# An MM-DiT block on one core: the first stage rebuilt (scale columns and V weights loaded in interleaved row pieces, V accumulated in six open banks, layernorm on two engines), and the text branch's modulation moved from the Q stage to the K stage

## Chip, cores, metric

One core of a Trainium2 chip. The metric is the time of one execution in microseconds (us), as the device reports it; lower is better. Times are medians over all runs of a job; ratios use its fast-state runs alone. The span of a profile is about 2 us shorter than the reported time.

## The reference, cut to what matters

```python
B, Ni, Nt, D = 2, 256, 32, 1152            # bf16
mod_i = silu(c) @ wmod_img                 # shift, scale, gate columns of the image branch
mod_t = silu(c) @ wmod_txt                 # the same for the text branch
hi = layernorm(x_img) * (1 + sci) + shi
ht = layernorm(x_txt) * (1 + sct) + sht
qkvi, qkvt = hi @ wqkv_img, ht @ wqkv_txt
p = softmax(concat(qt, qi) @ concat(kt, ki).T * D ** -0.5)
a = p @ concat(vt, vi)
out_i = x_img + gai * (ai @ wo_img)
out_t = x_txt + gat * (at @ wo_txt)
```

All 14 weight blocks of 1152 x 1152 (2.65 MB each, 37.2 MB) are read once; with the activations and the scratch rows the profile counts 39.5 MB read from HBM.

## The kernel before: what the change and the argument touch

There are three things to know. First, the image branch: layernorm, transposes on TensorE, a pass that multiplies by the scale (three engines), then V, then shift, then Q, then K.

```python
w_sc_i = load_w(wmod_img, D)                              # one DMA of 2.65 MB each
w_v_i = load_w(wqkv_img, 2 * D, splits=(CH, 2 * CH))      # by columns
w_sh_i = load_w(wmod_img, 0)
w_q_i = load_w(wqkv_img, 0)
w_sh_t = load_w(wmod_txt, 0)                              # text shift, text scale ...
w_sc_t = load_w(wmod_txt, D)
w_k_i = load_w(wqkv_img, D)                               # ... ahead of the image K weights
# [cut]
for i in range(NIT):
    layernorm(x_i[:, i, :], P, xn_i[:, i, :])             # VectorE statistics, ScalarE sqrt
    ... transposes, ScalarE copies the result to hT_i
for b in range(B):
    h_pass(b, shift=False)                                # hT_i *= 1 + scale, three engines
```

Second, the text branch's shift and scale are computed as rows (`mod_rows`). A row has to reach 64 partitions. The kernel stores it to a scratch tensor in DRAM and reads it back broadcast. Both DMAs are issued by GpSimd:

```python
def mod_rows(w_blk, si, add_one=False, lhs=None):
    ...                                                   # 36 matmuls, PSUM copied to g_sb
    for b in range(B):
        nc.gpsimd.dma_start(gsc[si, b, :]..., g_sb[b:P:32, :])          # store
def txt_rows_scale():
    mod_rows(w_sc_t, 1, add_one=True)
    for k in range(2):                                    # k = 0 shift, k = 1 scale
        for b in range(B):
            nc.gpsimd.dma_start(mb_t[b * NT:(b + 1) * NT, k, :], gsc[k, b, :].partition_broadcast(NT))
def txt_modulate():                                       # VectorE
    mul(xn_t, xn_t, mb_t[:, 1, :]); add(xn_t, xn_t, mb_t[:, 0, :])
def txt_transposes(): ...                                 # TensorE, 9 transposes, then hT_t
```

Third, where these pieces stand among the nine groups of nine matmuls that make up Q and K:

```python
qk_img(w_q_i, 0, hooks={0: txt_ln, 3: txt_rows_shift, 6: txt_rows_scale})
qk_img(w_k_i, 1, hooks={5: txt_modulate, 7: txt_transposes})
```

## Time and profile before

| | before |
|---|---|
| time, median of 3 | 130.49 us |
| span of the profile | 128.9 us |
| TensorE (PE) busy | 110.3 us, 86% |
| Q's first matmul | 40.4 us |
| K's last group ends | 78.6 us |

The second part of the page shows the span in 40 equal slices: TensorE's busy share in tenths, the granted TensorE clock in tenths, and the DMA traffic in GB/s.

```profile
PE   0005799999999999999999999799989999999960
PEclk9999999999999999999999999999999999999999
GB/s 59 409 415 357 381 401 406 409 411 412 357 405 411 406 409 410 408 413 379 412 371 372 372 374 374 388 412 405 409 405 411 335 14 90 6 92 0 92 97 46
```

TensorE has nothing to do for 11 us and then is busy to the end. The loads run near 400 GB/s to about 100 us. So the kernel is bound by TensorE, after a start that waits for x, layernorm and the first scale columns.

The chain of waits (start, length, what), from Q to the end of the text branch, shows a TensorE that never waits for the text branch:

```profile
40.46 2.05 PE ps L218 x9
...
74.29 0.36 PE tpt L293 x9
...
75.25 3.40 PE ps L218 x15
78.65 4.32 PE ps L305 x148
82.96 0.93 issue
```

L218 is the Q and K matmuls, L293 the text transposes, L305 the text Q and K. The timeline of GpSimd shows the trips through DRAM; L259 is a store to scratch and L279 a read-back:

```profile
48.41 1.15 POOL L259 DMA_DIRECT2D mod_scratch<-g_sb  x2 [0.50 <-DVE g_sb L129]
53.44 1.09 POOL L279 DMA_DIRECT2D mb_t<-mod_scratch  x2 [3.88 <-DMA mod_scratch<-g_sb]
55.56 1.17 POOL L259 DMA_DIRECT2D mod_scratch<-g_sb  x2 [1.03 <-DVE g_sb L253]
61.27 1.15 POOL L279 DMA_DIRECT2D mb_t<-mod_scratch  x2 [4.54 <-DMA mod_scratch<-g_sb]
```

The scale rows' matmuls end at 54.8 us. The store is issued at 55.6, the read-back at 61.3, and its data are in at 66.9 (the later of the two copies). The text transposes stand at 74.2 in TensorE's order, so some 6 us of slack are left after 1.5 us of VectorE work.

### The profile page before, as it was taken

The numbers are of one execution on the slowest core, as the hardware profiler recorded it, in microseconds if no ns is written. First come the engines' busy times: TensorE is split into PE (matmuls) and PEld (weight loads), VectorE is DVE, ScalarE is ACT, GpSimd is POOL, SyncE is SP. The second block draws the span as 40 slices with busy tenths as digits, with TensorE's granted clock in tenths as the row PEclk, the third lists the DMA queues.
The fourth block names the chain that finished last, engine by engine and source line by source line (L and its number), as shares of the span: only waits on it lengthen the run. The fifth ranks groups of instructions, "written<-read, shape, count | busy, mean of one in ns | idle before, by whom it ended". The sixth has DMA issues, their size and how long they took to land.

```text
span 128.9 us, 2643 instructions
## 1 busy us (share of the span) xinstructions
PE 110.3 (86%) x1123; PEld 69.3 (54%) x1128; DVE 56.7 (44%) x147; ACT 33.4 (26%) x71; POOL 19.8 (15%) x48
## 2 busy tenths in 40 slices
PE   0005799999999999999999999799989999999960
PEld 0004685665865454544444447778767755555550
DVE  0099965111357610231026211225987656545670
ACT  3054584221133211101111031143675400010000
POOL 8910132000034133330300000011200000000000
PEclk9999999999999999999999999999999999999999
DMA  3999999999999999999999999999999802020221
GB/s 59 409 415 357 381 401 406 409 411 412 357 405 411 406 409 410 408 413 379 412 371 372 372 374 374 388 412 405 409 405 411 335 14 90 6 92 0 92 97 46
DMA packets 19703, 41.05 MB, mean 318 GB/s; under 512 B 811, under 2 KB 3403, under 8 KB 19691
## 3 DMA queue, kind: packets, MB, share of 16 engines
q1 hardware_dynamic: 18875, 39.75, 81.7%
q0 software_dynamic: 672, 1.06, 2.2%
q8 instruction: 9, 0.15, 0.5%
q10 hardware_dynamic: 144, 0.07, 0.2%
q14 instruction: 3, 0.02, 0.0%
HBM read 39.53 MB, written 1.35 MB: 317 GB/s over the span
## 4 chain that ended last, share of the span: by engine, by line
PE 79%; DVE 8%; DMA 4%; ACT 3%; issue 2%; DVEq 0%
PE ps L218 27%; PE ps L227 14%; PE ps L426 14%; PE aps L377 5%; PE gps L249 5%; DMA x_i<-in_x_img_dram 4%; PE ps L305 4%; PE tp L158 3%; PE mps L164 2%; DVE stats L142 2%; PE ps L446 2%; PE sps L336 2%; ACT hT_i L159 1%; DVE pb L328 1%; DVE pb L326 1%
## 5 line engine op out<-in xcount | busy, mean ns | idle before, releaser
L218 PE MATMUL ps<-hT_i,t 128*128 128x512 bf16 x157 | 35.4, 379 | 0.3
L218 PEld LDWEIGHTS <-t 128*128 128x128 bf16 x162 | 15.5, 98 | 18.9 <-issue 0.7
L227 PE MATMUL ps<-t,hT_i 128*128 128x384 bf16 x108 | 18.9, 338 | 0.0
L426 PE MATMUL ps<-t,aT 128*128 128x384 bf16 x108 | 17.9, 326 | 0.0
L227 PEld LDWEIGHTS <-hT_i 128*128 128x128 bf16 x108 | 10.9, 102 | 7.4 <-issue 0.3
L426 PEld LDWEIGHTS <-aT 128*128 128x128 bf16 x108 | 10.6, 98 | 6.8
L429 DVE TENSOR_TENSOR tmp<-ps,gb 128x384 bf16<-128x384 f32 x12 | 6.7, 558 | 7.3 <-PE ps L426 7.3
L129 DVE CAST qkT<-ps 128x512 bf16<-128x512 f32 (+1 forms) x5 | 3.3, 665 | 13.6 <-PE ps L218 11.8
L118 PE MATMUL sT_ps<-ident,s_140 18*128 18x18 bf16 x1 | 0.2, 192 | 10.5 <-DVE s_140 L116 10.5
L259 POOL DMA_DIRECT2D mod_scratch<-g_sb x8 | 4.7, 591 | 27.4 <-DVE g_sb L129 26.4
L129 DVE CAST v_i<-ps 128x384 bf16<-128x384 f32 x6 | 3.3, 557 | 11.5 <-PE ps L227 11.5
L205 DVE TENSOR_SCALAR qkT<-ps 128x512 bf16<-128x512 f32 (+1 forms) x5 | 3.3, 665 | 11.5 <-PE ps L218 8.7
L131 ACT CAST qkT<-ps 128x512 bf16<-128x512 f32 (+1 forms) x6 | 3.3, 542 | 19.5 <-PE ps L218 16.4
L142 DVE BATCH_NORM_STATS2 stats<-x_i 128x6 f32<-128x384 bf16 x12 | 5.9, 531 | 5.3 <-DMA x_i<-in_x_img_dram 5.3
L207 ACT ACTIVATE qkT<-ps 128x512 bf16<-128x512 f32 (+1 forms) x6 | 3.3, 553 | 17.9 <-PE ps L218 16.2
L377 PE MATMUL aps<-pT,v_i 128*128 128x288 bf16 x36 | 6.6, 286 | 0.7 <-ACT pT L131 0.6
L182 DVE TENSOR_SCALAR hT_i<-hT_i,mod_img 128x256 bf16<-128x256 bf16 x20 | 5.8, 346 | 0.7 <-ACT hT_i L159 0.6
L305 PE MATMUL ps<-hT_t,t 128*128 128x64 bf16 x162 | 5.0, 193 | 0.9 <-issue 0.9
L118 PEld LDWEIGHTS <-s_140 18*128 18x128 bf16 x1 | 0.1, 100 | 10.5 <-DVE s_140 L116 10.5
L158 PE MATMUL tp<-ident,xn_i 128*128 128x128 bf16 x36 | 4.5, 310 | 1.3 <-DVE xn_i L148 0.9
L305 PEld LDWEIGHTS <-t 128*128 128x128 bf16 x162 | 4.9, 98 | 1.3 <-issue 1.0
L159 ACT COPY hT_i<-tp 128x640 bf16<-128x640 bf16 (+1 forms) x8 | 4.7, 642 | 2.8 <-PE tp L158 2.8
(88 smaller groups left out, 127.0 us busy)
## 6 DMA issues: line engine op xcount, KB each, us to landing
t<-in_wmod_img_dram SPq DMA_DIRECT2D x3, 2592.0 KB, 17.8
t<-in_wmod_txt_dram SPq DMA_DIRECT2D x3, 2592.0 KB, 16.9
t<-in_wqkv_txt_dram SPq DMA_DIRECT2D x3, 2592.0 KB, 24.1
t<-in_wqkv_img_dram SPq DMA_DIRECT2D x2, 2592.0 KB, 22.1
t<-in_wo_img_dram SPq DMA_DIRECT2D x1, 2592.0 KB, 23.5
t<-in_wo_txt_dram SPq DMA_DIRECT2D x1, 2592.0 KB
t<-in_wqkv_img_dram SPq DMA_DIRECT2D x1, 1728.0 KB, 16.5
x_i<-in_x_img_dram SPq DMA_DIRECT2D x1, 1152.0 KB, 5.5
```

The source lines that it names most:

```text
L129: last_dve[0] = nc.vector.tensor_copy(out_ap, in_ap)
L142: nc.vector.bn_stats(stats[0:np_, k, :], x_ap[:, k * CH:(k + 1) * CH])
L158: nc.tensor.transpose(tp[:, kt - k0, :], xn_i[:, i, kt * P:(kt + 1) * P], ident[:])
L159: nc.scalar.copy(hT_i[:, k0:k1, i * P:(i + 1) * P], tp[:, 0:k1 - k0, :])
L182: nc.vector.tensor_scalar(sl, sl, ap, None, op0=op)
L218: nc.tensor.matmul(ps[:], lhsT=wq[:, kt, j * P:(j + 1) * P], rhs=hT_i[:, kt, :], start=(kt == 0), stop=(kt == KT - 1))
L227: nc.tensor.matmul(ps[:], lhsT=hT_i[:, kt, i * P:(i + 1) * P], rhs=w_v_i[:, kt, cch * CH:(cch + 1) * CH], start=(kt == 0), stop=(kt == KT ...
L249: nc.tensor.matmul(gps[32 * g:32 * g + 32, :], lhsT=lhs[:, kt, :], rhs=w_blk[:, kt, g * VC:(g + 1) * VC], start=(kt == 0), stop=(kt == KT ...
L305: nc.tensor.matmul(ps[:, j - j0, :], lhsT=wq[:, kt, j * P:(j + 1) * P], rhs=hT_t[:, kt, :], start=(kt == 0), stop=(kt == KT - 1))
L377: nc.tensor.matmul(aps[:], lhsT=lhsT, rhs=pT[:, kj, :], start=(kj == 0), stop=(kj == 2))
L426: nc.tensor.matmul(ps[0:np_, :], lhsT=lhsT_of(dt), rhs=w_o[:, dt, cs], start=(dt == 0), stop=(dt == KT - 1))
L429: nc.vector.tensor_mul(tmp[0:np_, :], ps[0:np_, :], gate_ap[:, cs])
```

## The change

The intent is to start V earlier. Scale columns and V rows arrive in alternating pieces. As soon as a piece of scale columns is known, the transposed tokens are scaled while they leave PSUM. V accumulates piece by piece in six PSUM banks that stay open. Layernorm is shared between ScalarE and VectorE, dummy matmuls should raise TensorE's clock beforehand, and the order of TensorE is fixed ("pinned"). The new scaled copy takes room, so weight buffers go from six to five. K's weights now come ahead of the text weights, and with them the text rows move into K. The diff, cut to its core:

```diff
-    wpool = ctx.enter_context(tc.tile_pool(name="w", bufs=6))
+    wpool = ctx.enter_context(tc.tile_pool(name="w", bufs=5))
-    ps_mm = ... bufs=4 ; ps_tr bufs=2 ; ps_sm bufs=2
+    ps_mm = ... bufs=6 ; ps_tr bufs=2
+    pin = tc.keep_in_program_order          # every matmul and transpose; the first stage's other work
-    w_sc_i = load_w(wmod_img, D)
-    w_v_i = load_w(wqkv_img, 2 * D, splits=(CH, 2 * CH))
+    KCH = [(0, 2), (2, 5), (5, KT)]
+    for (k0, k1), ksplit in zip(KCH, KSP):
+        nc.sync.dma_start(w_sc_i[:, :, k0 * P:k1 * P], sc_v[:, :, k0 * P:k1 * P])
+        for (a0, a1) in ksplit:
+            nc.sync.dma_start(w_v_i[:, a0:a1, :], v_v[:, a0:a1, :])
     w_sh_i = load_w(wmod_img, 0)
     w_q_i = ...
+    w_k_i = load_w(wqkv_img, D)
     nc.sync.dma_start(x_t[:], xt_flat[:, :])
     w_sh_t = load_w(wmod_txt, 0)
     w_sc_t = load_w(wmod_txt, D)
-    w_k_i = load_w(wqkv_img, D)
# ... [cut: silu and rstd by exp/ln, layernorm of row tiles 0 and 2 on ScalarE]
+    warm_up(8); ... warm_up(5)              # dummy matmuls before and after c's transpose
+    mods(*KCH[0])                           # first scale columns
+    warm_up(3)
+    transposes(*KCH[0], 0)                  # evacuated with * (1 + scale)
+    ln_sq(s2, ...); m3 = ln_stats(...)      # statistics of the second pair of row tiles
+    v_open(A0, *KCH[0]) ... v_open(...)     # V, 512 wide, row piece by row piece
# ... [cut: shift added by 18 VectorE instructions into a second copy]
-    qk_img(w_q_i, 0, hooks={0: txt_ln, 3: txt_rows_shift, 6: txt_rows_scale})
+    qk_img(w_q_i, 0)
-    qk_img(w_k_i, 1, hooks={5: txt_modulate, 7: txt_transposes})
+    qk_img(w_k_i, 1, hooks={0: txt_ln, 1: txt_rows_shift, 3: txt_rows_scale, 7: txt_modulate, 8: txt_transposes})
```

More of the change, by code (lines that the diff above doesn't have):

```diff
@@ L53, with mm, tr @@
     small = ctx.enter_context(tc.tile_pool(name="small", bufs=4))
-    ps_mm = ctx.enter_context(tc.tile_pool(name="ps_mm", bufs=4, space=PSUM))
+    ps_mm = ctx.enter_context(tc.tile_pool(name="ps_mm", bufs=6, space=PSUM))
     ps_tr = ctx.enter_context(tc.tile_pool(name="ps_tr", bufs=2, space=PSUM))
-    ps_sm = ctx.enter_context(tc.tile_pool(name="ps_sm", bufs=2, space=PSUM))
+    pin = tc.keep_in_program_order
+    def mm(*a, **k):
+        return pin(nc.tensor.matmul(*a, **k))
+    def tr(*a, **k):
+        return pin(nc.tensor.transpose(*a, **k))
     xi_flat = x_img.rearrange("b n d -> (b n) d")
@@ L61, with wtile, wview @@
     ot_flat = out_1.rearrange("b n d -> (b n) d")
+    KCH = [(0, 2), (2, 5), (5, KT)]
+    KSP = [[(0, 1), (1, 2)], [(2, 5)], [(5, 7), (7, KT)]]
     x_i = act.tile([P, NIT, D], bf)
-    nc.sync.dma_start(x_i[:], xi_flat.rearrange("(i p) d -> p i d", p=P))
     c18 = small.tile([B * KT, P], bf, bufs=1)
-    nc.sync.dma_start(c18[:], c.rearrange("b (kt p) -> (b kt) p", p=P))
+    nc.scalar.dma_start(c18[:], c.rearrange("b (kt p) -> (b kt) p", p=P))
     x_t = act.tile([NTT, D], bf)
+    def wtile():
+        return wpool.tile([P, KT, D], bf, tag="w", name="t")
+    def wview(src, c0):
+        return src.rearrange("(kt p) n -> p kt n", p=P)[:, :, c0:c0 + D]
     def load_w(src, c0, splits=(D,)):
-        t = wpool.tile([P, KT, D], bf, tag="w")
-        sv = src.rearrange("(kt p) n -> p kt n", p=P)
+        t = wtile()
+        sv = wview(src, c0)
         o = 0
         for n in splits:
-            nc.sync.dma_start(t[:, :, o:o + n], sv[:, :, c0 + o:c0 + o + n])
+            nc.sync.dma_start(t[:, :, o:o + n], sv[:, :, o:o + n])
             o += n
         return t
-    w_sc_i = load_w(wmod_img, D)
-    w_v_i = load_w(wqkv_img, 2 * D, splits=(CH, 2 * CH))
+    w_sc_i = wtile()
+    w_v_i = wtile()
+    sc_v, v_v = wview(wmod_img, D), wview(wqkv_img, 2 * D)
+    for i in range(NIT):
+        nc.sync.dma_start(x_i[:, i, :], xi_flat[i * P:(i + 1) * P, :])
+    for (k0, k1), ksplit in zip(KCH, KSP):
+        nc.sync.dma_start(w_sc_i[:, :, k0 * P:k1 * P], sc_v[:, :, k0 * P:k1 * P])
+        for (a0, a1) in ksplit:
+            nc.sync.dma_start(w_v_i[:, a0:a1, :], v_v[:, a0:a1, :])
     w_sh_i = load_w(wmod_img, 0)
-    w_q_i = load_w(wqkv_img, 0)
+    w_q_i = load_w(wqkv_img, 0, splits=(CH, 2 * CH))
+    w_k_i = load_w(wqkv_img, D)
     nc.sync.dma_start(x_t[:], xt_flat[:, :])
@@ L92, with warm_up @@
     w_o_t = load_w(wo_txt, 0)
+    nc.scalar.preload_act_table_set("natural_log_exp_and_others")
+    eps_t = const.tile([P, 1], f32)
+    nc.vector.memset(eps_t[:], EPS)
+    warm = const.tile([P, 512], bf)
+    nc.vector.memset(warm[:], 0.0)
     ident = const.tile([P, P], bf)
     make_identity(nc, ident[:])
-    eps_t = const.tile([P, 1], f32)
-    nc.vector.memset(eps_t[:], EPS)
+    wps = ps_mm.tile([P, 512], f32, tag="mm")
+    def warm_up(n):
+        for _ in range(n):
+            mm(wps[:], lhsT=warm[:, 0:P], rhs=warm[:], start=True, stop=True)
+    warm_up(8)
+    sT32 = const.tile([P, KT, 32], bf)
+    nc.gpsimd.memset(sT32[:], 0.0)
+    shT32 = const.tile([P, KT, 32], bf)
+    nc.gpsimd.memset(shT32[:], 0.0)
+    v_t = act.tile([P, B, D], bf)
+    nc.gpsimd.memset(v_t[:], 0.0)
     selF = const.tile([P, 2, 2, B, NT], bf)
@@ L103, with silu_cols @@
                 nc.gpsimd.tensor_copy(selF[:, r, g, b, :], ident[:, col:col + 1].to_broadcast([P, NT]))
-    sT32 = const.tile([P, KT, 32], bf)
-    nc.gpsimd.memset(sT32[:], 0.0)
-    shT32 = const.tile([P, KT, 32], bf)
-    nc.gpsimd.memset(shT32[:], 0.0)
-    v_t = act.tile([P, B, D], bf)
-    nc.gpsimd.memset(v_t[:], 0.0)
     e18 = small.tile([B * KT, P], f32, bufs=1)
-    nc.scalar.activation(e18[:], c18[:], ACT.Exp, scale=-1.0)
-    nc.vector.tensor_scalar_add(e18[:], e18[:], 1.0)
-    nc.vector.reciprocal(e18[:], e18[:])
+    pin(nc.scalar.activation(e18[:], c18[:], ACT.Exp, scale=-1.0))
+    pin(nc.scalar.activation(e18[:], e18[:], ACT.Ln, bias=1.0))
+    pin(nc.scalar.activation(e18[:], e18[:], ACT.Exp, scale=-1.0))
     s18 = small.tile([B * KT, P], bf, bufs=1)
-    nc.vector.tensor_mul(s18[:], c18[:], e18[:])
-    sT_ps = ps_sm.tile([P, B * KT], bf, tag="sm")
-    nc.tensor.transpose(sT_ps[:], s18[:], ident[0:B * KT, 0:B * KT])
+    pin(nc.vector.tensor_mul(s18[:], c18[:], e18[:]))
+    sT_ps = ps_tr.tile([P, B * KT], bf, tag="tr")
+    tr(sT_ps[:], s18[:], ident[0:B * KT, 0:B * KT])
     sT = const.tile([P, KT, B], bf)
-    nc.vector.tensor_copy(sT[:], sT_ps[:].rearrange("p (b kt) -> p kt b", b=B))
-    nc.vector.tensor_copy(sT32[:, :, 0:B], sT[:])
+    warm_up(5)
+    def silu_cols():
+        pin(nc.vector.tensor_copy(sT[:], sT_ps[:].rearrange("p (b kt) -> p kt b", b=B)))
+        nc.gpsimd.tensor_copy(sT32[:, :, 0:B], sT[:])
     evac_idx = [0]
@@ L137, in after_last_dve, with ln_stats @@
                           reason="keep long-latency op behind psum evacuations")
-    def layernorm(x_ap, np_, out_ap):
+    def ln_stats(x_ap, np_, between=None):
         stats = small.tile([P, NCH, 6], f32, tag="stats")
         for k in range(NCH):
-            nc.vector.bn_stats(stats[0:np_, k, :], x_ap[:, k * CH:(k + 1) * CH])
+            if k == 1 and between:
+                between()
+            pin(nc.vector.bn_stats(stats[0:np_, k, :], x_ap[:, k * CH:(k + 1) * CH]))
         mv = small.tile([P, 2], f32, tag="mv")
-        nc.vector.bn_aggr(mv[0:np_, :], stats[0:np_, :, :])
-        rstd = small.tile([P, 1], f32, tag="rstd")
-        nc.scalar.activation(rstd[0:np_, :], mv[0:np_, 1:2], ACT.Sqrt, bias=eps_t[0:np_, :])
-        nc.vector.reciprocal(rstd[0:np_, :], rstd[0:np_, :])
-        nc.vector.tensor_scalar(out_ap, x_ap, mv[0:np_, 0:1], rstd[0:np_, :], op0=ALU.subtract, op1=ALU.mult)
@@ L150 @@
-    xn_i = act.tile([P, NIT, D], bf, tag="A")
-    hT_i = act.tile([P, KT, B * NI], bf, tag="Bt")
-    KSPL = [(0, 5), (5, KT)]
-    for i in range(NIT):
-        layernorm(x_i[:, i, :], P, xn_i[:, i, :])
-        for (k0, k1) in KSPL:
-            tp = ps_tr.tile([P, 5, P], bf, tag="tr")
-            for kt in range(k0, k1):
-                nc.tensor.transpose(tp[:, kt - k0, :], xn_i[:, i, kt * P:(kt + 1) * P], ident[:])
-            nc.scalar.copy(hT_i[:, k0:k1, i * P:(i + 1) * P], tp[:, 0:k1 - k0, :])
+        pin(nc.vector.bn_aggr(mv[0:np_, :], stats[0:np_, :, :]))
@@ new lines, in ln_stats, with ln_sum, ln_sq, ln_var @@
+        return mv
+    def ln_sum(x_ap, junk):
+        sm = small.tile([P, 3], f32, tag="lnact")
+        pin(nc.scalar.activation(junk, x_ap, ACT.Copy, scale=1.0 / D, accum_out=sm[:, 0:1]))
+        return sm
+    def ln_sq(sm, x_ap, junk):
+        pin(nc.scalar.activation(junk, x_ap, ACT.Square, scale=float(D) ** -0.5, accum_out=sm[:, 1:2]))
+    def ln_var(sm):
+        pin(nc.vector.scalar_tensor_tensor(sm[:, 2:3], sm[:, 0:1], sm[:, 0:1], sm[:, 1:2],
+                                           op0=ALU.mult, op1=ALU.subtract))
@@ new lines, in ln_rstd, with ln_norm @@
+    def ln_rstd(var, np_, sign=1.0):
+        rstd = small.tile([P, 1], f32, tag="rstd")
+        pin(nc.scalar.activation(rstd[0:np_, :], var, ACT.Ln, bias=eps_t[0:np_, :], scale=sign))
+        pin(nc.scalar.activation(rstd[0:np_, :], rstd[0:np_, :], ACT.Exp, scale=-0.5))
+        return rstd
+    def ln_norm(x_ap, mean, rstd, np_, out_ap):
+        pin(nc.vector.tensor_scalar(out_ap, x_ap, mean, rstd[0:np_, :], op0=ALU.subtract, op1=ALU.mult))
+    xn_i = act.tile([P, NIT, D], bf, tag="A")
+    hS_i = act.tile([P, KT, B * NI], bf, tag="Bt")
@@ L161, in mod_cols @@
+    hT_i = act.tile([P, KT, B * NI], bf)
+    mod_i = const.tile([P, 2 * KT, B], f32, name="mod_img")
+    qkT = act.tile([P, 2 * KT, B, NTOK], bf, tag="Q")
     def mod_cols(wt, out_ps, j0, j1):
@@ L163, in mod_cols @@
             for kt in range(KT):
-                nc.tensor.matmul(out_ps[:, j - j0, :], lhsT=wt[:, kt, j * P:(j + 1) * P], rhs=sT[:, kt, :],
-                                 start=(kt == 0), stop=(kt == KT - 1))
-    qkT = act.tile([P, 2 * KT, B, NTOK], bf, tag="Q")
-    mod_i = const.tile([P, 2 * KT, B], f32, name="mod_img")
-    for (j0, j1) in [(0, 3), (3, 6), (6, KT)]:
-        mps = ps_sm.tile([P, KT, B], f32, tag="sm")
-        mod_cols(w_sc_i, mps, j0, j1)
-        nc.vector.tensor_scalar_add(mod_i[:, KT + j0:KT + j1, :], mps[:, 0:j1 - j0, :], 1.0)
@@ L174 @@
-    mod_eng = [0, 1, 0, 2, 0, 1, 0, 2, 0]
-    def h_pass(b, shift):
-        for kt in range(KT):
-            sl = hT_i[:, kt, b * NI:(b + 1) * NI]
-            ap = mod_i[:, kt, b:b + 1] if shift else mod_i[:, KT + kt, b:b + 1]
-            op = ALU.add if shift else ALU.mult
-            if mod_eng[kt] == 0:
-                nc.vector.tensor_scalar(sl, sl, ap, None, op0=op)
-            elif mod_eng[kt] == 1:
-                if shift:
-                    nc.gpsimd.tensor_scalar(sl, sl, 1.0, ap, op0=ALU.mult, op1=ALU.add)
-                else:
-                    nc.gpsimd.tensor_scalar(sl, sl, ap, 0.0, op0=ALU.mult, op1=ALU.add)
-            elif shift:
-                nc.scalar.activation(sl, sl, ACT.Identity, bias=ap, scale=1.0)
-            else:
-                nc.scalar.activation(sl, sl, ACT.Identity, scale=ap)
@@ L193, with mods @@
-    for b in range(B):
-        h_pass(b, shift=False)
-    def mod_shift_img():
-        mps = ps_sm.tile([P, KT, B], f32, tag="sm")
-        mod_cols(w_sh_i, mps, 0, KT)
-        nc.vector.tensor_copy(mod_i[:, 0:KT, :], mps[:])
-        nc.vector.tensor_copy(shT32[:, :, 0:B], mps[:])
+                mm(out_ps[:, j - j0, :], lhsT=wt[:, kt, j * P:(j + 1) * P], rhs=sT[:, kt, :],
+                   start=(kt == 0), stop=(kt == KT - 1))
+    def mods(k0, k1):
+        mps = ps_tr.tile([P, KT, B], f32, tag="tr")
+        mod_cols(w_sc_i, mps, k0, k1)
+        pin(nc.vector.tensor_scalar_add(mod_i[:, KT + k0:KT + k1, :], mps[:, 0:k1 - k0, :], 1.0))
@@ new lines, with transposes @@
+    sc_idx = [0]
+    def transposes(k0, k1, b):
+        tp = ps_tr.tile([P, 4, NI], bf, tag="tr")
+        for kt in range(k0, k1):
+            for t in range(TPB):
+                i = b * TPB + t
+                tr(tp[:, kt - k0, t * P:(t + 1) * P], xn_i[:, i, kt * P:(kt + 1) * P], ident[:])
+        for kt in range(k0, k1):
+            dst, src, ap = hS_i[:, kt, b * NI:(b + 1) * NI], tp[:, kt - k0, :], mod_i[:, KT + kt, b:b + 1]
+            if sc_idx[0] % 2 == 0:
+                pin(nc.vector.tensor_scalar(dst, src, ap, None, op0=ALU.mult))
+            else:
+                pin(nc.scalar.activation(dst, src, ACT.Copy, scale=ap))
+            sc_idx[0] += 1
@@ new lines, with v_open @@
+    VW = 512
+    v_i = act.tile([P, NIT, D], bf, tag="A")
+    accs = {}
+    def v_open(ids, k0, k1, kt_major=True):
+        for key in ids:
+            if key not in accs:
+                accs[key] = ps_mm.tile([P, VW], f32, tag="mm", name="vps")
+        loop = [(kt, key) for kt in range(k0, k1) for key in ids] if kt_major else \
+            [(kt, key) for key in ids for kt in range(k0, k1)]
+        for kt, (i, cc) in loop:
+            mm(accs[(i, cc)][:], lhsT=hS_i[:, kt, i * P:(i + 1) * P], rhs=w_v_i[:, kt, cc * VW:(cc + 1) * VW],
+               start=(kt == 0), stop=(kt == KT - 1), skip_group_check=True)
+            if kt == KT - 1:
+                evac(v_i[:, i, cc * VW:(cc + 1) * VW], accs[(i, cc)][:])
@@ new lines, with ln_norm_dve, ln_norm_act @@
+    A0 = [(0, 0), (1, 0), (0, 1), (1, 1)]
+    A1 = [(2, 0), (3, 0)]
+    def ln_norm_dve(i, mv):
+        ln_norm(x_i[:, i, :], mv[:, 0:1], ln_rstd(mv[:, 1:2], P), P, xn_i[:, i, :])
+    def ln_norm_act(i, sm):
+        ln_norm(x_i[:, i, :], sm[:, 0:1], ln_rstd(sm[:, 2:3], P, sign=-1.0), P, xn_i[:, i, :])
+    s0 = ln_sum(x_i[:, 0, :], xn_i[:, 0, :])
+    ln_sq(s0, x_i[:, 0, :], xn_i[:, 0, :])
+    m1 = ln_stats(x_i[:, 1, :], P, between=silu_cols)
+    ln_var(s0)
+    ln_norm_dve(1, m1)
+    ln_norm_act(0, s0)
@@ new lines @@
+    s2 = ln_sum(x_i[:, 2, :], xn_i[:, 2, :])
+    mods(*KCH[0])
+    warm_up(3)
+    transposes(*KCH[0], 0)
+    ln_sq(s2, x_i[:, 2, :], xn_i[:, 2, :])
+    m3 = ln_stats(x_i[:, 3, :], P)
+    ln_var(s2)
+    ln_norm_dve(3, m3)
+    ln_norm_act(2, s2)
+    v_open(A0, *KCH[0])
+    transposes(*KCH[0], 1)
+    mods(*KCH[1])
+    transposes(*KCH[1], 0)
+    v_open(A1, *KCH[0])
+    transposes(*KCH[1], 1)
+    v_open(A0, *KCH[1])
+    mods(*KCH[2])
+    transposes(*KCH[2], 0)
+    v_open(A1, *KCH[1])
@@ new lines @@
+    transposes(*KCH[2], 1)
+    v_open(A0, *KCH[2], kt_major=False)
+    v_open(A1, *KCH[2], kt_major=False)
+    v_open([(2, 1), (3, 1)], 0, KT, kt_major=False)
+    mps = ps_tr.tile([P, KT, B], f32, tag="tr")
+    mod_cols(w_sh_i, mps, 0, KT)
+    nc.vector.tensor_copy(mod_i[:, 0:KT, :], mps[:])
+    nc.vector.tensor_copy(shT32[:, :, 0:B], mps[:])
+    for kt in range(KT):
+        for b in range(B):
+            nc.vector.tensor_scalar(hT_i[:, kt, b * NI:(b + 1) * NI], hS_i[:, kt, b * NI:(b + 1) * NI],
+                                    mod_i[:, kt, b:b + 1], None, op0=ALU.add)
@@ L202, in qk_evac @@
+    vps = ps_mm.tile([P, NIT, P], f32, tag="mm")
+    for i in range(NIT):
+        for kt in range(KT):
+            mm(vps[:, i, :], lhsT=hS_i[:, kt, i * P:(i + 1) * P], rhs=w_v_i[:, kt, 2 * VW:D],
+               start=(kt == 0), stop=(kt == KT - 1))
+    evac(v_i[:, :, 2 * VW:D], vps[:])
     def qk_evac(out_ap, in_ap, blk):
@@ L217, in qk_img @@
             for kt in range(KT):
-                nc.tensor.matmul(ps[:], lhsT=wq[:, kt, j * P:(j + 1) * P], rhs=hT_i[:, kt, :],
-                                 start=(kt == 0), stop=(kt == KT - 1))
+                mm(ps[:], lhsT=wq[:, kt, j * P:(j + 1) * P], rhs=hT_i[:, kt, :],
+                   start=(kt == 0), stop=(kt == KT - 1))
             qk_evac(qkT[:, blk * KT + j, :, 0:NI], ps[:].rearrange("p (b n) -> p b n", b=B), blk)
-    v_i = act.tile([P, NIT, D], bf, tag="A")
-    def v_group(i, cch):
-        ps = ps_mm.tile([P, CH], f32, tag="mm")
-        for kt in range(KT):
-            nc.tensor.matmul(ps[:], lhsT=hT_i[:, kt, i * P:(i + 1) * P], rhs=w_v_i[:, kt, cch * CH:(cch + 1) * CH],
-                             start=(kt == 0), stop=(kt == KT - 1))
-        evac(v_i[:, i, cch * CH:(cch + 1) * CH], ps[:])
-    v_order = [(i, 0) for i in range(NIT)]
-    for b in range(B):
-        v_order += [(b * TPB + t, cch) for t in range(TPB) for cch in range(1, NCH)]
-    V_HOOK = 9
-    for n, (i, cch) in enumerate(v_order):
-        if n == V_HOOK:
-            mod_shift_img()
-            h_pass(0, shift=True)
-        v_group(i, cch)
     NGG = 4
@@ L248, in mod_rows @@
             for g in range(NGG):
-                nc.tensor.matmul(gps[32 * g:32 * g + 32, :], lhsT=lhs[:, kt, :], rhs=w_blk[:, kt, g * VC:(g + 1) * VC],
+                mm(gps[32 * g:32 * g + 32, :], lhsT=lhs[:, kt, :], rhs=w_blk[:, kt, g * VC:(g + 1) * VC],
                                  start=(kt == 0), stop=(kt == KT - 1), tile_position=(0, 32 * g))
@@ L259, in mod_rows @@
             nc.gpsimd.dma_start(gsc[si, b, :].rearrange("(g j) -> g j", g=NGG), g_sb[b:P:32, :])
-    h_pass(1, shift=True)
     mod_rows(w_v_i, 4, lhs=shT32)
@@ L269, in txt_ln @@
     def txt_ln():
-        layernorm(x_t[:, :], NTT, xn_t[:, :])
+        mv = ln_stats(x_t[:, :], NTT)
+        ln_norm(x_t[:, :], mv[0:NTT, 0:1], ln_rstd(mv[0:NTT, 1:2], NTT), NTT, xn_t[:, :])
     def txt_rows_shift():
@@ L292, in txt_transposes @@
         for kt in range(KT):
-            nc.tensor.transpose(tpt[:, kt, :], xn_t[:, kt * P:(kt + 1) * P], ident[0:NTT, 0:NTT])
+            tr(tpt[:, kt, :], xn_t[:, kt * P:(kt + 1) * P], ident[0:NTT, 0:NTT])
         nc.scalar.copy(hT_t[:], tpt[:])
-    qk_img(w_k_i, 1, hooks={5: txt_modulate, 7: txt_transposes})
+    qk_img(w_k_i, 1, hooks={0: txt_ln, 1: txt_rows_shift, 3: txt_rows_scale, 7: txt_modulate, 8: txt_transposes})
     FG = 6
@@ L304 @@
                 for kt in range(KT):
-                    nc.tensor.matmul(ps[:, j - j0, :], lhsT=wq[:, kt, j * P:(j + 1) * P], rhs=hT_t[:, kt, :],
+                    mm(ps[:, j - j0, :], lhsT=wq[:, kt, j * P:(j + 1) * P], rhs=hT_t[:, kt, :],
                                      start=(kt == 0), stop=(kt == KT - 1))
@@ L335, in scores_img @@
             for ft in range(KT):
-                nc.tensor.matmul(sps[:], lhsT=qkT[:, ft, b, q0:q0 + P], rhs=qkT[:, KT + ft, b, :],
+                mm(sps[:], lhsT=qkT[:, ft, b, q0:q0 + P], rhs=qkT[:, KT + ft, b, :],
                                  start=(ft == 0), stop=(ft == KT - 1))
@@ L343, in scores_txt @@
             for b in range(B):
-                nc.tensor.matmul(sps[NT * b:NT * (b + 1), :], lhsT=qkT[:, ft, b, NI:NTOK], rhs=qkT[:, KT + ft, b, :],
+                mm(sps[NT * b:NT * (b + 1), :], lhsT=qkT[:, ft, b, NI:NTOK], rhs=qkT[:, KT + ft, b, :],
                                  start=(ft == 0), stop=(ft == KT - 1), tile_position=(0, NT * b))
@@ L355, in p_transposes @@
             for kj in range(3):
-                nc.tensor.transpose(pT_ps[:, kj, qp:qp + P], pb[:, kj * P:(kj + 1) * P], ident[:])
+                tr(pT_ps[:, kj, qp:qp + P], pb[:, kj * P:(kj + 1) * P], ident[:])
         qp = qpos[b][2]
@@ L360, in p_transposes @@
         for kj in range(3):
-            nc.tensor.transpose(pT_ps[:, kj, qp:qp + NT], pb[r0:r0 + NT, kj * P:(kj + 1) * P],
+            tr(pT_ps[:, kj, qp:qp + NT], pb[r0:r0 + NT, kj * P:(kj + 1) * P],
                                 ident[r0:r0 + NT, r0:r0 + NT])
@@ L376, in attn_out @@
                     lhsT = v_t[:, b, dt * P:(dt + 1) * P]
-                nc.tensor.matmul(aps[:], lhsT=lhsT, rhs=pT[:, kj, :], start=(kj == 0), stop=(kj == 2))
+                mm(aps[:], lhsT=lhsT, rhs=pT[:, kj, :], start=(kj == 0), stop=(kj == 2))
             evac(aT[:, dt, b * NTOK:(b + 1) * NTOK], aps[:])
@@ L385, in v_txt @@
                     c0 = (2 * r + g) * VC
-                    nc.tensor.matmul(ps[64 * g:64 * g + NTT, :], lhsT=hT_t[:, kt, :], rhs=w_v_t[:, kt, c0:c0 + VC],
+                    mm(ps[64 * g:64 * g + NTT, :], lhsT=hT_t[:, kt, :], rhs=w_v_t[:, kt, c0:c0 + VC],
                                      start=(kt == 0), stop=(kt == KT - 1), tile_position=(0, 64 * g))
@@ L415, in txt_gate @@
             bps = ps_mm.tile([P, VC], f32, tag="mm")
-            nc.tensor.matmul(bps[:], lhsT=selF[:, r, :, :, :].rearrange("p g b t -> p (g b t)"), rhs=g_sb[:],
+            mm(bps[:], lhsT=selF[:, r, :, :, :].rearrange("p g b t -> p (g b t)"), rhs=g_sb[:],
                              start=True, stop=True)
@@ L425, in out_tile @@
             for dt in range(KT):
-                nc.tensor.matmul(ps[0:np_, :], lhsT=lhsT_of(dt), rhs=w_o[:, dt, cs],
+                mm(ps[0:np_, :], lhsT=lhsT_of(dt), rhs=w_o[:, dt, cs],
                                  start=(dt == 0), stop=(dt == KT - 1))
@@ L445 @@
                 c0 = (2 * r + g) * VC
-                nc.tensor.matmul(ps[64 * g:64 * g + NTT, :], lhsT=aT[:, dt, NI:NI + NTT], rhs=w_o_t[:, dt, c0:c0 + VC],
+                mm(ps[64 * g:64 * g + NTT, :], lhsT=aT[:, dt, NI:NI + NTT], rhs=w_o_t[:, dt, c0:c0 + VC],
                                  start=(dt == 0), stop=(dt == KT - 1), tile_position=(0, 64 * g))
```

## The prediction

> **What bounds the kernel now.** Busy rows: TensorE 86% of the 128.9 us span; chain of waits: 79% on it. From 18.5 us (first V matmul, timeline) to 88 us TensorE has one visible gap, 0.9 us. First transposes run at 11.0. Loads run at 405 GB/s in most slices but sit ahead of use: Q weights landed near 33 us, first read at 40.4; K weights near 53 and 60.4. A gain at the start can pay one for one.
>
> **What changes at the start.** (a) x arrives in four pieces, statistics are split over ScalarE and VectorE: by the traced costs (530 ns a statistic, 570 ns a normalize) the first pair of row tiles is normalized near 9.2 us instead of 12.1, the second near 14.3 instead of 16.1. (b) Warm-up matmuls. The traced transposes are spaced 127 ns and the first V matmuls 320 ns, later ones 163 to 175: the array starts at half clock. The Trainium skill, "TensorE: Matmul & The Clock Gate", Part 1, says the same (about 3.4 us of activity release the clock); the trace agrees. Warm, I estimate 36 transposes at about 65 ns, saving 2 us, and V saving 1 us. (c) V in 512-wide pieces: 72 x 0.216 + 36 x about 0.06 = 17.7 us against 18.6 traced. (d) Lost: TensorE waits about 1.7 us for the second normalized pair. (e) The shift is now 18 adds on VectorE alone (286 ns each, 5.1 us, before on three engines), beginning after the shift columns, about 3.3 us before Q can start: Q's first group stalls about 1 us. Q starts in effect near 38.1 us instead of 40.5: 2.4 us gained. Transposes, columns, V and rows are still some 26 us of TensorE work.
>
> **What it costs later.** Text shift and scale rows move from Q to K (groups 1 and 3), the text transposes stand before K group 8. Between the scale rows' end and the transposes lie five groups, 9.7 us. The chain they need is in the trace: rows end 54.8, store to scratch issued 55.6, read back issued 61.3, landed about 66.4, then multiply and add 1.5 us: 13.2 us.  So TensorE should stand idle 3.6 us before the text transposes, 1 us more if GpSimd issues the shift's read-back first, more if the clock falls. I count 3.3 us; the hops may be shorter.
>
> With five weight buffers instead of six the loads should remain ahead: the slots of the early weights come free by about 65 us. After K nothing on the chain changes.
>
> **Sum.** 130.5 - 2.4 + 3.3 = 131.4 us; I say 131.2, range 127.0 to 134.0. Faster by over 2% 0.22, within 2% 0.57, slower by over 2% 0.21.
>
> **What would show it.** Right: Q's first matmul near 37 to 38 us; transposes at 60 to 70 ns; V done near 32; in K a TensorE gap of 3 to 5 us ahead of the text transposes, released by the multiply/add that waited for the scratch read-back; loads continuous to about 100 us. Wrong: Q's start later than 39.5 (start gain not there); no gap in K; a gap ahead of gate rows or Q because a weight buffer came late.
>
> **What would make it wrong.** The scratch hops take 2 to 3 us instead of 5: then the front gain shows in full, 128 us or lower. Or the idle time in K drops the clock: 133 or more.

## The result

| | before | changed |
|---|---|---|
| time, median (4 runs each) | 130.45 us | 135.58 us |
| span of the profile | 128.9 us | 133.3 us |
| Q's first matmul | 40.4 | 38.3 |
| text transposes start | 74.2 | 79.7 |
| text Q and K start | 78.5 | 83.8 |
| gate rows start (next stage) | 84.4 | 88.6 |

The ratio is 1.0379, with a 95% interval of 1.0314 to 1.0445: slower. A ratio here is the mean time of one kernel's fast runs over that of the other kernel's fast runs of the same rounds, so it is not quite the ratio of the medians quoted. The time lies outside the predicted range of 127.0 to 134.0.

The same rows of the page of the changed kernel:

```profile
PE   6828999999999999999999209999979999989960
PEclk9975799999999999999999955999999999999996
GB/s 150 263 357 345 394 406 404 412 381 402 405 410 306 406 410 412 411 411 409 407 419 375 411 386 234 111 409 406 410 400 386 390 74 15 73 88 0 93 88 44
```

Two slices of the PE row read 2 and 0, at 73 to 80 us. In the next two the granted clock is at half. The chain of waits shows what stands there (L60 is now the line of all matmuls, L63 that of all transposes; L345 is the store, L365 the read-back):

```profile
60.25 5.28 DMA mod_scratch<-g_sb
...
66.08 1.03 POOL mb_t L365 x2
67.11 0.33 POOL mod_scratch L345
...
68.27 4.10 issue
...
72.38 0.52 POOL mb_t L365
...
72.99 4.95 DMA mb_t<-mod_scratch
...
78.07 0.76 DVE xn_t L373
...
78.86 0.76 DVE xn_t L374
...
79.66 0.66 PE tpt L63 x9
```

The 4.10 us called "issue" are the second store on its way; the profile did not name it there. The timeline of TensorE has the same gap from its own side: 5.48 us idle, and after it matmuls of the last K group at half clock.

```profile
64.30 9.89 PE L60 MATMUL ps<-hT_i,t 128*128 128x512 bf16 x44
79.66 0.66 PE L63 MATMUL tpt<-ident,xn_t 64*128 64x64 bf16 x9 [5.48 <-DVE xn_t L374]
...
81.08 2.83 PE L60 MATMUL ps<-hT_i,t 128*128 128x512 bf16 x7 [0.22 <-issue]
83.75 4.89 PE L60 MATMUL ps<-hT_t,t 128*128 128x64 bf16 x162
```

The sum, from the starts in the two timelines. Start of Q: 38.34 - 40.39 = -2.05 us. The gap: +5.5. Transposes and last K group: 83.75 - 79.66 = 4.1 us where 2.3 would do at the pace before (0.36 + 1.94), so +1.8. The 0.93 us gap in the text matmuls of before is gone: -0.9. Together +4.3, and the spans differ by 4.4.

The DMA hole at about 81 to 86 us (slices of 234 and 111 GB/s) is a consequence. With five buffers, the image output weights wait for the K weights' buffer, which the late K group frees late (their load is issued at 83.9 us). Those weights are used only from 107 us.

### The profile page after: what moved, and what is told of

It reads as the page before. It is cut to its first block, busy times and chain, and to the rows that moved or that the text cites. A ratio compares the mean times of both kernels' runs of the same rounds, so it can differ in the third digit from the quotient of the medians.

```text
span 133.3 us, 2669 instructions
## 1 busy us (share of the span) xinstructions
PE 116.3 (87%) x1136; PEld 68.4 (51%) x1144; DVE 54.6 (41%) x140; ACT 32.6 (24%) x75; POOL 15.4 (12%) x41
## 4 chain that ended last, share of the span: by engine, by line
PE 71%; DMA 13%; issue 5%; DVE 4%; POOL 2%; ACT 1%; SPq 1%; POOLq 0%; DVEq 0%
PE ps L60 37%; PE vps L60 14%; DMA t<-in_wmod_img_dram 5%; PE aps L60 5%; PE sps L60 4%; DMA mod_scratch<-g_sb 4%; DMA mb_t<-mod_scratch 4%; PE mps L60 3%; PE gps L60 3%; PE tp L63 2%; SPq L96 1%; POOL mb_t L365 1%; PE wps L60 1%; PE pT_ps L63 1%; POOL mod_scratch L345 1%
## 5 line engine op out<-in xcount | busy, mean ns | idle before, releaser
L60 PEld LDWEIGHTS <-t 128*128 128x128 bf16 x486 | 25.3, 98 | 24.5 <-DMA t<-in_wmod_img_dram 3.6
L60 PE MATMUL ps<-hT_i,t 128*128 128x512 bf16 x157 | 36.8, 389 | 0.4 <-issue 0.2
L60 PE MATMUL ps<-t,aT 128*128 128x384 bf16 (+1 forms) x144 | 20.2, 316 | 0.0
L60 PE MATMUL vps<-t,hS_i 128*128 128x512 bf16 (+1 forms) x105 | 19.6, 341 | 0.6 <-DVE hS_i L233 0.4
L60 PEld LDWEIGHTS <-aT 128*128 128x128 bf16 (+1 forms) x144 | 12.5, 101 | 7.3 <-issue 0.3
L60 PEld LDWEIGHTS <-hS_i 128*128 128x128 bf16 x108 | 9.2, 101 | 9.0 <-issue 1.7
L345 POOL DMA_DIRECT2D mod_scratch<-g_sb x8 | 4.7, 586 | 62.1 <-ACT g_sb L165 48.2
L310 DVE TENSOR_SCALAR qkT<-ps 128x512 bf16<-128x512 f32 (+1 forms) x6 | 3.8, 636 | 15.3 <-PE ps L60 15.3
L60 PE MATMUL aps<-pT,v_i 128*128 128x288 bf16 x36 | 6.7, 286 | 0.9 <-ACT v_t L165 0.9
L60 PE MATMUL mps<-sT,t 128*128 128x2 bf16 x162 | 4.7, 164 | 3.1 <-DMA t<-in_wmod_img_dram 3.1
L60 PE MATMUL wps<-warm 128*128 128x512 bf16 x16 | 6.3, 550 | 1.2 <-DVE warm L119 1.2
L235 ACT ACTIVATE hS_i<-tp,mod_img 128x256 bf16<-128x256 bf16 x9 | 4.3, 473 | 10.3 <-DVE hS_i L233 9.9
L60 PE MATMUL sps<-qkT 128*128 128x288 bf16 (+1 forms) x54 | 5.8, 286 | 0.0
L63 PE MATMUL tpt<-ident,xn_t 64*128 64x64 bf16 x9 | 0.7, 237 | 5.5 <-DVE xn_t L374 5.5
L60 PE MATMUL aps<-pT,v_t 128*128 128x288 bf16 x18 | 5.1, 286 | 0.1
L60 PE MATMUL gps<-t,sT_139 128*32 128x288 bf16 x144 | 5.1, 287 | 0.0
## 6 DMA issues: line engine op xcount, KB each, us to landing
t<-in_wqkv_txt_dram SPq DMA_DIRECT2D x3, 2592.0 KB, 19.3
```

Source lines behind the costliest of these rows:

```text
L60: return pin(nc.tensor.matmul(*a, **k))
L63: return pin(nc.tensor.transpose(*a, **k))
L235: pin(nc.scalar.activation(dst, src, ACT.Copy, scale=ap))
L310: nc.vector.tensor_scalar_mul(out_ap, in_ap, SCALE)
L345: nc.gpsimd.dma_start(gsc[si, b, :].rearrange("(g j) -> g j", g=NGG), g_sb[b:P:32, :])
```

## The experiments

Theory A: the new start gains about 2 us; the text chain through DRAM, put into K with five groups (9.7 us) to hide in, costs more than that. Rivals: five weight buffers or the pinned order (B); the place of the text rows and weights by itself (C); the clock.

### e1: the text part put back, the new start kept

```diff
+    nc.sync.dma_start(x_t...); w_sh_t = ...; w_sc_t = ...   # back ahead of
     w_k_i = load_w(wqkv_img, D)
-    qk_img(w_q_i, 0)
+    qk_img(w_q_i, 0, hooks={0: txt_ln, 3: txt_rows_shift, 6: txt_rows_scale})
-    qk_img(w_k_i, 1, hooks={0: txt_ln, 1: ..., 3: ..., 7: txt_modulate, 8: txt_transposes})
+    qk_img(w_k_i, 1, hooks={5: txt_modulate, 7: txt_transposes})
```

> The changed kernel with only the text part put back as it was before: text layernorm and row matmuls in the Q stage, modulate and transposes at K groups 5 and 7, and the text shift and scale weights loaded before the image K weights. Theory A (the loss is the text chain moved into K): Q's first matmul stays near 38.4 us, no TensorE gap over 0.5 us in K, K's last matmul near 76.6 us instead of 83.5 (changed) and 78.6 (before); time about 128.2 us. Rival B (five buffers, the pinned order or the colder clock at the start cost the time): still above 132 us.

Measured: 128.07 us against 130.65 in the same rounds, ratio 0.9779 (0.9715 to 0.9843), correct. Its chain of waits runs through TensorE without a break from Q's start:

```profile
38.78 5.93 PE ps L60 x27
...
53.09 19.53 PE ps L60 x90
72.62 0.37 PE tpt L63 x9
72.98 8.71 PE ps L60 x180
```

Everything else of the change is still in: five buffers, pins, warm-ups, the clock at the start. So B can't be the loss. The whole loss sits in the moved text part, and the rest is a gain of about 2%.

### e2: the same order, but no trip through DRAM

```diff
-  nc.gpsimd.dma_start(mb_t[..., k, :], gsc[k, b, :].partition_broadcast(NT))
+  nc.gpsimd.dma_start(mb_t[..., k, :], c[b, :].partition_broadcast(NT))   # wrong on purpose
```

> The changed kernel, everything in place, but the text modulation reads its two rows from an input (c) instead of from the scratch rows just stored: wrong text output on purpose, image output wrong through the text keys too. Same TensorE work in the same order, same loads. Theory A (TensorE waits for the store and read-back through DRAM): the 5.5 us gap before the text transposes goes, group 8 of K takes 1.9 us instead of 3.3 and the time falls by about 7 us, to 128 to 129. Rival C (the placement of row matmuls and weights in K costs by itself): the time stays above 132.

Measured: 128.6 us, ratio 0.9816 (0.9747 to 0.9885). Its output is wrong, which doesn't matter for the time. The run that was profiled counts as slow, so only its structure is used here: the gap before the text transposes is 0.28 us and the last K group takes 1.95 us (76.60 to the text matmuls at 78.56):

```profile
76.24 0.43 PE L63 MATMUL tpt<-ident,xn_t 64*128 64x64 bf16 x9 [0.28 <-DVE xn_t L374]
76.60 2.12 PE L60 MATMUL ps<-hT_i,t 128*128 128x512 bf16 x9
```

The copies of c were issued from 5.4 us on and had landed by 13.4, so this run takes out both trips and the order of GpSimd's queue at once; e6 tells them apart. Rows, weights and hooks are where the changed kernel has them. It is the wait for the scratch trip, not the place as such, that costs; C falls.

### e4: the text part alone, in the kernel before

> The kernel before with only the text part of the change: K weights loaded before the text shift and scale weights, text layernorm and rows in K groups 0, 1 and 3, modulate and transposes at 7 and 8. Theory A: the loss alone, without the gain at the start: a TensorE gap of 4 to 6 us before the text transposes, and 5 to 7 us slower than before, 135.5 to 137.5. Rival B: within 1 us of before.

The edit is the reverse of e1's, applied to the kernel before. Measured: 137.71 us against 130.65, ratio 1.0529 (1.0438 to 1.0621), correct. The timeline has the gap (4.86 us) and the half-clock group after it (nine matmuls in 3.8 us, up to 85.78):

```profile
66.63 9.89 PE L218 MATMUL ps<-hT_i,t 128*128 128x512 bf16 x45
81.38 0.66 PE L293 MATMUL tpt<-ident,xn_t 64*128 64x64 bf16 x9 [4.86 <-DVE xn_t L288]
81.97 4.02 PE L218 MATMUL ps<-hT_i,t 128*128 128x512 bf16 x9
```

The text part alone costs 7.1 us (137.71 - 130.65). The changed kernel loses 5.1, and the 2 us between are the gain at the start.

### e5: the kernel before with five weight buffers

```diff
-tc.tile_pool(name="w", bufs=6)
+tc.tile_pool(name="w", bufs=5)
```

> The kernel before with five weight buffers instead of six. If the loads keep ahead of use with five (theory): within 0.5 us of before. If five buffers are part of the loss: over 1 us slower, with TensorE waits for a weight load.

Measured: 130.1 us against 131.2, ratio 0.9949 (0.9884 to 1.0015), the same. TensorE waits for no weight. Five buffers are not part of the loss.

### e6: the read-back of the shift row issued by another engine

In the changed kernel GpSimd's queue holds, in the order of the trace (the source lists both read-backs last): store shift, read back shift, store scale, read back scale. The second entry waits for the first to land. The scale rows' matmuls were done at 64.4 us, but the scale store was issued only at 67.1.

```diff
-  nc.gpsimd.dma_start(mb_t[..., k, :], gsc[k, b, :]...)
+  (nc.scalar if k == 0 else nc.gpsimd).dma_start(mb_t[..., k, :], gsc[k, b, :]...)
```

> The changed kernel with the read-back of the text shift row issued by ScalarE, so that GpSimd's queue holds only stores and the scale row's read-back. In the changed kernel GpSimd stood waiting for the shift store to land until 66.1 us and issued the scale store only at 67.1, 2.7 us after the scale rows' matmuls ended (64.4), where the kernel before needed 0.8. If that queue order is the part of the gap that I mis-sized: scale store issued near 65.2, TensorE gap about 3.5 us instead of 5.5; if the gap is then short enough for the clock to hold, group 8 of K takes 1.95 us. Time 132 to 134. If the hops themselves lengthened: gap still above 5 us, time above 135.

Measured: 133.4 us against 131.2, ratio 1.0177 (1.0127 to 1.0227), correct: about 2 points less loss than the changed kernel's 1.0379. The timelines of GpSimd and TensorE in this run:

```profile
59.33 1.15 POOL L345 DMA_DIRECT2D mod_scratch<-g_sb  x2 [13.74 <-DVE g_sb L163]
64.25 1.13 POOL L345 DMA_DIRECT2D mod_scratch<-g_sb  x2 [3.77 <-DVE g_sb L339]
69.44 0.52 POOL L365 DMA_DIRECT2D mb_t<-mod_scratch  x1 [4.06 <-DMA mod_scratch<-g_sb]
```

```profile
63.38 9.89 PE L60 MATMUL ps<-hT_i,t 128*128 128x512 bf16 x45
76.86 0.43 PE L63 MATMUL tpt<-ident,xn_t 64*128 64x64 bf16 x9 [3.60 <-DVE xn_t L374]
77.23 3.15 PE L60 MATMUL ps<-hT_i,t 128*128 128x512 bf16 x9
```

The scale store now leaves 0.8 us after the rows (64.25 against 63.45), and the gap is 3.60 us instead of 5.48. So 1.9 us of the gap were the order of GpSimd's queue; 3.6 us are what the rest of the chain, the two hops (store and read-back) above all, takes beyond the cover. The clock fell after 3.6 us of idling too: nine matmuls took 2.9 us (77.23 to the text matmuls at 80.17) instead of 1.95.

### e3 and e3b: dummy matmuls in the gap

```diff
+        for _ in range(24):                  # e3b: 18
+            mm(wps2[:], lhsT=warm[:, 0:P], rhs=warm[:], start=True, stop=True)
         tpt = ps_tr.tile([P, KT, NTT], bf, tag="tr")
```

> The changed kernel with 24 dummy matmuls (5.2 us warm) set before the text transposes, inside the gap, into a spare bank. If the gap also costs by letting the TensorE clock fall to half: the gap's length stays, the last K group takes 1.95 us instead of 3.3, mean clock rises from 0.94 to about 0.97 and the time falls by about 1.4 us. If the lower clock costs nothing, no change (0 to 0.3 us).

> Repeat of e3 with 18 dummy matmuls instead of 24 in the gap. e3 had the last K group at full clock (1.95 us, not 3.3) but its scratch read-back landed 1.4 us later, so its time did not fall. If that later landing was chance: the gap ends near 79.5 again and the time falls by 1.0 to 1.4 us against the changed kernel, to 134.2 to 134.6. If filling the gap lengthens the hop each time: no change, 135.2 to 136.

Measured, e3: 135.37 us, ratio 1.0361 (1.0288 to 1.0433), against 1.0379 for the changed kernel: no gain. The last K group did run at full clock (1.95 us, 81.75 to 83.70), so the low clock does cost 1.5 us of TensorE time there (in the changed kernel the group took 3.5 us, 80.25 to 83.75). But the transposes started at 81.4 instead of 79.7, because the last read-back took 6.4 us from issue to landing, not 4.9 to 5.0:

```profile
81.38 0.43 PE L63 MATMUL tpt<-ident,xn_t 64*128 64x64 bf16 x9 [1.87 <-DVE xn_t L374]
81.75 2.12 PE L60 MATMUL ps<-hT_i,t 128*128 128x512 bf16 x9
```

All four runs of e3 took 135.2 to 135.9 us, at mean clocks of 0.968 to 0.985 against 0.941 and 0.942 in the changed kernel, which starts alike. So the clock was probably held in all four and something took the gain back in all four; only one was traced. e3b does not settle why: three of its four runs count as slow (136.06 to 137.69), one as fast (133.04, in other rounds 2.0 us below the changed kernel's lowest). In its profiled slow run the hop was again 6.4 us; there the 18 dummies left 2.81 us uncovered, the clock fell within that gap (at 78.7 us), and the last K group took 3.8 us. The kernel before also had one hop of 6.4. Whether filler matmuls lengthen the hop or both profiles met a long hop by chance stays open.

### f1, f2, f3: the warm-ups and the order of the first stage, on top of e1

The prediction gave the warm-up matmuls about 3 us. The TensorE timeline of the changed kernel shows why that is doubtful:

```profile
1.23 3.59 PE L60 MATMUL wps<-warm 128*128 128x512 bf16 x8 [1.23 <-DVE warm L119]
4.88 1.25 PE L60 MATMUL wps<-warm 128*128 128x512 bf16 x5
9.26 0.64 PE L60 MATMUL mps<-sT,t 128*128 128x2 bf16 x18 [3.12 <-DMA t<-in_wmod_img_dram]
9.76 1.44 PE L60 MATMUL wps<-warm 128*128 128x512 bf16 x3
10.99 0.63 PE L63 MATMUL tp<-ident,xn_i 128*128 128x128 bf16 x4
12.07 3.40 PE L60 MATMUL vps<-t,hS_i 128*128 128x512 bf16 x8 [0.45 <-DVE hS_i L233]
15.40 0.40 PE L63 MATMUL tp<-ident,xn_i 128*128 128x128 bf16 x4
```

The first 13 dummies do reach full clock (5 in 1.25 us). Then TensorE idles 3.1 us until the first scale columns land, the clock falls (in the record at 8.3 us), and the first eight V matmuls take 3.40 us, twice their later time. They hide behind the layernorm of the second pair of row tiles, which ends at 15.3. The third warm-up (3 dummies, 1.3 us at half clock) stands in front of the first transposes. The statistics of the second pair stand behind their evacuation in the pinned order.

f1 takes out all 16 dummies:

> The repaired kernel (changed kernel with the text part back, e1) without any of the 16 warm-up matmuls. My prediction held that warm-up saves about 3 us. The trace of the changed kernel shows the clock falling again at about 10 us, after 3.1 us without a matmul, and the first 8 V matmuls at half clock, but hidden behind the second pair's layernorm. Theory (warm-up is worth nothing there, the third batch even delays the transposes by 1.3 us): Q's first matmul at 37.4 to 38.7 us against 38.7 in e1, time within 1 us of 128.1, more likely 0.5 to 1.3 us faster. Rival (warm-up pays): 1 to 3 us slower, 129 to 131.

f2 takes out only the last 3:

> e1 without only the third warm-up (3 matmuls, 1.3 us at half clock, between the first scale columns and the first transposes). If the first transposes wait for it: they start near 10.2 us instead of 11.3, and as the second pair's statistics stand behind the first scaled evacuation in both engines' order, the second pair is normalized about 1.1 us earlier; Q's first matmul about 1 us earlier, near 37.7, time about 127.1. If something else ends last there: no change.

f3 moves the second pair's statistics forward, lengthens the second warm-up to 18 and drops the third:

> e1 with the second pair's statistics moved ahead of the first scaled evacuation (in program order, which is pinned), the second warm-up lengthened from 5 to 18 matmuls so that TensorE stays busy until the scale columns land, the third warm-up taken out. Expected: second pair normalized near 12.2 us instead of 15.3, first V matmuls at full clock (215 ns, not 425), Q's first matmul 1.5 to 2 us earlier than in e1, near 36.9; the last V rows landing near 22 us then become the limit. Time about 126.3. If the rows of V already were the limit: no change.

| same rounds, before 130.7 us | time | ratio (95%) | Q's first matmul |
|---|---|---|---|
| f1 | 127.97 us | 0.9780 (0.9742 to 0.9818) | 36.9 |
| f2 | 127.37 us | 0.9724 (0.9682 to 0.9767) | 37.4 |
| f3 | 127.39 us | 0.9757 (0.9719 to 0.9794) | 38.6 |

e1, in its own rounds, had 0.9779 and Q at 38.7. Without any warm-up nothing is lost. f2 has the lowest ratio, but its interval overlaps those of f1 and f3. In f2's profile the 13 dummies never reached full clock (they are 0.43 us apart to the last one), unlike in the changed kernel, and nothing was lost by it. f3 got what it was built for and no more: its V began at full clock (8 matmuls in 1.9 us) and the second pair was transposed at 13.0. Then the second piece of scale columns ended TensorE's wait (0.75 us). The clock still fell, though only after that wait: the record has it at half from 15.9 to 19.3 us, and the V matmuls in that stretch start 0.43 us apart. The timeline up to the wait:

```profile
10.98 1.90 PE L60 MATMUL vps<-t,hS_i 128*128 128x512 bf16 x8 [0.47 <-DVE hS_i L233]
13.01 0.40 PE L63 MATMUL tp<-ident,xn_i 128*128 128x128 bf16 x4
14.16 0.83 PE L60 MATMUL mps<-sT,t 128*128 128x2 bf16 x27 [0.75 <-DMA t<-in_wmod_img_dram]
```

The starts of Q in this table carry some chance: the first scale columns arrived at 8.8 us in the profiled runs of f1 and f2, and at about 9.6 in those of e1 and f3.

### f4: the scale weight whole, not interleaved, on top of e1

```diff
+    nc.sync.dma_start(w_sc_i[:], sc_v)
     for (k0, k1), ksplit in zip(KCH, KSP):
-        nc.sync.dma_start(w_sc_i[:, :, k0 * P:k1 * P], sc_v[:, :, k0 * P:k1 * P])
         for (a0, a1) in ksplit:
```

> e1 with the scale weight loaded whole ahead of V's row pieces, so not interleaved. The whole scale weight lands near 13.2 us (it did in the kernel before). If the interleave pays: first scaled evacuation near 13.7 us instead of 11.7, Q's first matmul 1.5 to 3 us later than in e1, time 129.6 to 131. If layernorm and TensorE work set the pace anyway: within 0.7 us of 128.1.

Measured: 133.76 us against 130.7, ratio 1.0232 (1.0192 to 1.0272), correct, so 4.5 points worse than e1, nearly 6 us. I had expected 1.5 to 3 us. TensorE waited 9.0 us for the scale weight, to 14.8 us, and every later step of the first stage moved by the same 5 us:

```profile
14.82 0.64 PE L60 MATMUL mps<-sT,t 128*128 128x2 bf16 x18 [9.02 <-DMA t<-in_wmod_img_dram]
...
16.55 0.63 PE L63 MATMUL tp<-ident,xn_i 128*128 128x128 bf16 x4
17.64 3.59 PE L60 MATMUL vps<-t,hS_i 128*128 128x512 bf16 x8 [0.45 <-DVE hS_i L233]
```

The kernel before transposed while the scale weight arrived (11.0 to 13.6 us) and scaled afterwards. With the scale in the evacuation, and the order pinned, nothing can go ahead of the scale columns. That form pays here only because the interleave brings the first columns at 9.3 us. What the other parts of the new start (open banks, layernorm on two engines, fixed order) earn by themselves was not tested.

## Why the prediction was wrong

It named the right mechanism and mis-sized it; the time (135.6) lies outside its range (to 134.0).

- **Start of Q.** Predicted a gain of 2.4 us; the profiles show 2.05, and e1 confirms a gain of that order. Its parts were less right. Warm-up counted 3 us and is worth nothing measurable (f1). The Q stall of 1 us from the shift adds (e) is hardly there: Q's first ten matmuls took 2.27 us. The wait for the second normalized pair, put at 1.7 us, was hidden under the half-clock V matmuls. Misses of opposite sign cancelled; that the sum came out near is in part luck.
- **The failed step: the gap in K.** "So TensorE should stand idle 3.6 us before the text transposes, 1 us more if GpSimd issues the shift's read-back first, more if the clock falls. I count 3.3 us". Both ifs happened, and I had counted neither. The idle time was 5.5 us: 3.6 us for the hops, the figure the prediction had worked out from the chain, and 1.9 us, not 1, for GpSimd's queue order (e6: gap 3.60 against 5.48). The first if could have been settled beforehand: the timeline of the kernel before already has the shift's read-back (53.44) ahead of the scale store (55.56). That step also supposed that "the hops may be shorter". They hardly were: 5.3 us from the scale store's issue (67.1) to the read-back's (72.4), and 5.6 from there to landing (78.0); before, 5.7 and 5.6 (the prediction read the landing as 66.4; it was 66.9). In e6 the store's hop took 5.2 us, so that one error of 0.5 us met another and 3.6 came out exactly is luck.
- **The clock after the gap** was named as a risk and given no time in the sum. The transposes and the last K group took 1.8 us longer; with a filler the group alone ran in 1.95 us instead of 3.5 (e3). Saving it did not shorten the kernel in e3, because the hop was longer there, and this part is open.
- **Right:** five buffers keep ahead in the old order (e5); loads continuous up to the gap, though not to 100 us, for the late K group made the hole after it; the gap released by the multiply and add that waited for the read-back.

In figures: predicted -2.4 + 3.3 = +0.9 us; measured by the timelines -2.05 + 5.5 + 1.8 - 0.9 = +4.3.

The Trainium skill, "TensorE: Matmul & The Clock Gate", section "Why this matters for your kernels", asks for no TensorE idle gaps over about 3 us. The traces agree only in part. The clock was at half after gaps of 3.1, 3.6 and 5.5 us, and the 0.84 us gap before the attention output in e1 and the 1.87 us gap in e3 left no such mark. But in the first stage it also fell around gaps of 1.8 us (f2, at 10.3 us), 2.0 us (e6, at 9.9 us) and 2.6 us (e3, at 9.2 us), and in f3 (at 15.9 us) with no gap above 0.75 us after its first dummy. So to stay under 3 us was not enough in these runs; why is not shown. A fall can also come late: in e6 the record has it at 78.2 us, 1.3 us after the gap had ended.

The prediction took from Part 1 of that page that some 3.4 us of activity releases the clock. In the profiled runs with dummies the recorded release came 2.9 us (f4) to 5.7 us (f2) after the first of them. In the kernel before, the V matmuls start 320 ns apart and later 163, so the array does start at half clock, but the change came at 20.6 us, 2.1 us after the first V matmul and 9.5 us after the first transpose: that trace did not show the 3.4 us. And the release must last until the work arrives; here a 3.1 us wait for data undid it.

## What to carry to other kernels

When a load or a branch is moved, list the latency chain that hangs on it (rows, store, read-back, elementwise, transposes) and count the independent TensorE work between its two ends: here 9.7 us of cover met a chain of 15.3 us, in an order that could not step aside. An in-order queue that holds a dependent read ahead of an independent store adds its wait to the chain, and the idle time comes with a second bill, the clock. The gain at the start, some 2 us, was real and is kept by leaving the branch where it had slack: f2 and f3, not told apart by their intervals, take 127.4 us, 2.4 to 2.8% below the kernel before by the ratios.

## What the Trainium skill lacked or had wrong

- "DMA: Bandwidth & Descriptors", "Anatomy of one DMA — SWDGE (gpsimd) path" gives a fixed cost of about 2.0 us for a DMA from GpSimd. Stores of 2.2 KB issued there took 5.2 us from issue to landing in the kernel before (median), and read-backs of 72 KB 4.9 to 6.4, beside a load stream of about 400 GB/s. The page's "Latency and other measured facts" has HBM latency rising under load, but gives no figure for such a small DMA beside a full load stream. With 2.0 us a hop the text branch would have seemed to fit in K (an estimate with that page's figure: 0.8 us to the store, two hops and 1.5 us of VectorE work make 6.3 us, under the 9.7 us of cover).
- "TensorE: Matmul & The Clock Gate", Part 1, warns that clock records can be unreliable. No page says this: up to its first recorded change the granted clock can read as full. The kernel before and f1 read 0.9 or more in their early slices (their first records begin at 20.6 and 14.6 us), while f1's first eight 512-wide V matmuls took 3.59 us, and nine transposes of the kernel before took 1.14 us (127 ns each), where the changed kernel later did six in 0.34 us. So the mean clocks 1.00 and 0.941 of the two kernels can't be compared; the spacing of matmuls can.
- No page has it: dummy matmuls that end 3.1 us before the real work bought nothing (f1 without them 127.97 us, e1 with them 128.07, in different rounds).
- No page says how much work within a stretch is enough to keep the clock: it fell around gaps of 1.8 to 2.6 us (f2, e6, e3), once with none above 0.75 us (f3), and held through one of 1.87 us (e3).
